# Giving out the split of a Wb tile between the two halves of a step's elementwise work

## The chip, the cores and the metric

One core of a Trainium2 chip runs the kernel. The time is device microseconds of one execution. Before the change three runs gave 1529.27, 1530.88 and 1530.9 us, with a median of 1530.88 us; less time is better. Five engines work in parallel, each through a queue of its own in program order: PE (matrix products), DVE and ACT and POOL (elementwise work), and SP, which here only issues transfers between the chip's memory and the on-chip buffers.

## The reference, cut to what matters

```python
# attention in two steps: the packed queries p attend to k and v, then q attends to the result
p_packed = sm_attn(p, k, v)
x = sm_attn(q, p_packed, p_packed)        # as 4608 tokens x 512
# first layer: d_ff = 2048
h = x @ w_in
P = a[0] + a[1] * h + a[2] * h**2 + a[3] * h**3
Q = 1.0 + abs(b[0]) * abs(h) + abs(b[1]) * h**2
x = (P / (Q + 1e-06)) @ w_out
# second layer: d_ff = 2048
h = x @ w2_in
out = (maximum(h, 0) + alpha * minimum(h, 0)) @ w2_out
```

The four weight matrices come as 64-bit floats, all else as 32-bit floats. Products are made exact enough by splitting each 32-bit operand into a rounded high part and a remainder (low part), and adding three products of parts.

## The kernel before, in words

The attention's last product is folded into the first layer's first weights: for each of the 8 batches, Wb = p_packed @ w_in, a matrix of 256 rows by 2048 columns, is made once and stored to the chip's memory (`wb_d`). The first layer then runs in 72 steps, 9 chunks of 512 tokens by 8 tiles of 256 columns: step g is chunk c = g // 8 and tile f = g % 8. A chunk takes its tokens from two batches (two "visits"), so it needs two Wb tiles in each step. Around them the loop from line 843 does, in program order:

- `emit_L1(g)` (line 591): 24 products on PE into `h`, a PSUM tile with two buffers. A buffer comes free for step g+2 when the last DVE operation of step g (L665) has read it.
- `emit_E1(g)` (line 631), the first half of the elementwise work: ACT makes `r_` = |h| (L642), `q_` (L643) and `v_` (L644) from h; POOL multiplies `q_` by `r_` (L645). For the step before, ACT copies its result into the high part of `gt` (L626) and POOL subtracts to make the low part (L627). DVE does L650 and L651 on `v_` and h.
- `emit_L2(g - 3)` (line 669): 24 products on PE of `gt` with w_out (L680), added up over a chunk in `acc`, which has one buffer.
- `emit_E2(g)` (line 653), the second half: ACT does a reciprocal square root (L657, which needs POOL's L645) and a square (L658, into h, after DVE's L651). At a chunk's end `emit_yo` copies `acc` out, one half on DVE (L614) and one on ACT (L616), and stores it on SP (L621); the next chunk's L2 waits for that. DVE ends with L663, L664, L665.
- `store_Wb()` and `next_wb(g)` (line 831).

The weights' conversion from 64 bits is hung onto these steps. A tile takes three operations on DVE (L89, L92, L95) and two on ACT (L84, L85). For w_out, steps 3 to 7 each do all three on DVE between L651 and L663, and steps 1 to 8 each split one tile (ACT L738, POOL L739) at the end of `emit_E2`. For the second layer's weights, from step 9 on, odd steps do L89 and even steps L92 and L95, at the same place; each fourth step (12, 16, 20 ...) also has four sums on POOL (L714) at its end, whose results SP stores (L719) early in the step after, ahead of a load (L707).

`next_wb(g)` holds the lines that the change touches. A Wb tile for step g+16 is asked for at the end of step g: `fetch_wb` (line 505) issues a load on SP (L511) into a staging tile `s`, one of three (tag `s2`, shared with the conversion), and the next step's `next_wb` calls `split_wb` (line 513): ACT copies the staged tile into the high part (L520), POOL subtracts for the low part (L521). 48 tiles go this way. In chunks 4 and 7 the tiles were kept from an earlier visit, and `split_wb` only issues a load of the parts on SP (L518); from step 65 on there is nothing left to split.

"Step s" below is the step whose first half is meant. The step's number isn't in the trace; `r__2042` is step 3, `r__3239` step 18.

Of the kernel before, what the change touches and what calls it, by code (L numbers as in the profile page):

```python
# [28 lines left out]
def attention_then_two_moes(ctx, tc, qT, kT, v, pT, w_in, w_out, ab, w2_in, w2_out, alpha, out):  # L29
# [69 lines left out]
    def open_pool(name, **kw):  # L99
        opened[name] = ExitStack()  # L100
        return opened[name].enter_context(tc.tile_pool(name=name, reuse_waits="tile", **kw))

    def close_pool(name):
        opened.pop(name).close()
# [87 lines left out]
    def wb_slot(n):  # L192
        return wp.tile([128, 2, 512], F32R, tag="C" if n // 8 % 2 else "B", name="wb")
# [243 lines left out]
    def store_Wb():  # L437
        while stores:
            bp, j, fc, t = stores.pop(0)
            for bi in range(2):  # L440
                nc.sync.dma_start(out=wb_d[2 * bp + bi][64 * j:64 * j + 64, 512 * fc - 512:512 * fc + 512],
                                  in_=t[64 * bi:64 * bi + 64, :])


    wb_t, whole_t, wb_q, nwb = {}, {}, [], [0]
# [46 lines left out]
    def load_a2(c):  # L492
        st = gp.tile([128, 2, CH], F32, tag="ast", name="ast", bufs=1)
        for _, b, o, n, t in chunks[c]:
            nc.sync.dma_start(out=st[:, :, o:o + n], in_=a2_d[b][:, :, t:t + n])
        a2_t[c] = st

    def split_a2(c):
        st = a2_t[c]
        t = spx.tile([128, 2, 2, CH], F32R, tag="a2t", name="a2t")  # L500
        act(t[:, 0], st, AF.Copy)
        pool.tensor_tensor(t[:, 1], st, t[:, 0], op=ALU.subtract)
        a2_t[c] = t

    def fetch_wb(n):
        v, f = divmod(n, NP)
        if v > VISITS.index(VISITS[v]):
            wb_q.append((v, f, None))
            return
        wb_q.append((v, f, s2_tile().rearrange("p (k f) -> p k f", k=2)))  # L510
        nc.sync.dma_start(out=wb_q[-1][2], in_=wb_d[VISITS[v]][:, 256 * f:256 * f + 256].rearrange("(k p) f -> p k f", p=128))  # L511

    def split_wb():
        v, f, st = wb_q.pop(0)
        whole = wb_slot(NP * v + f)
        t = whole.rearrange("p h (k f) -> p h k f", k=2)
        if st is None:
            nc.sync.dma_start(out=whole.bitcast(F32), in_=wbh_d[VISITS[v]][f])  # L518
        else:
            act(t[:, 0], st, AF.Copy)  # L520
            pool.tensor_tensor(t[:, 1], st, t[:, 0], op=ALU.subtract)  # L521
        wb_t[v, f] = t[:, 0], t[:, 1]
        whole_t[v, f] = whole

    def keep_wb(v, f):
        nc.sync.dma_start(out=wbh_d[VISITS[v]][f], in_=whole_t[v, f].bitcast(F32))
# [64 lines left out]
    def emit_L1(g):  # L591
        c, f = divmod(g, NP)
        h = psh.tile([128, 2, CH], F32, tag="h", name="h")
        for ft in range(2):
            for v, _, o, m, _ in chunks[c]:
                w = wb_t[v, f]
                n = 0
                for x, y in PASSES:
                    for k in range(2):
                        mm(h[:, ft, o:o + m], w[x][:, k, 128 * ft:128 * ft + 128], a2_t[c][:, y, k, o:o + m],  # L600
                           start=n == 0, stop=n == 5)
                        n += 1
        hps[g] = h
# [20 lines left out]
    def emit_hi(g):  # L624
        t = gt[g] = spa.tile([128, 2, 2, CH], F32R, tag="gt", name="gt", bufs=3)
        act(t[:, 0], vs[g], AF.Copy)  # L626
        pool.tensor_tensor(t[:, 1], vs.pop(g), t[:, 0], op=ALU.subtract)  # L627
# [3 lines left out]
    def emit_E1(s):  # L631


        late_step(s, "start")
        w2_step(s, "start")
        if s < NG:
            h = hps.pop(s)
            r_ = spa.tile([128, 2, CH], F32, tag="r_", name="r_", bufs=1)
            q_ = spa.tile([128, 2, CH], F32, tag="q_", name="q_", bufs=2)
            v_ = vs[s] = spa.tile([128, 2, CH], F32, tag="v_", name="v_", bufs=2)  # L640
            now[s] = h, r_, q_, v_
            act(r_, h, AF.Abs)  # L642
            act(q_, r_, AF.Identity, scale=b1, bias=b0)  # L643
            act(v_, h, AF.Identity, scale=a3, bias=a2c)  # L644
            pool.tensor_tensor(q_, q_, r_, op=ALU.mult)  # L645
        if 1 <= s <= NG:
            emit_hi(s - 1)
        late_step(s, "middle")
        if s < NG:
            dve.tensor_tensor(v_, v_, h, op=ALU.mult)  # L650
            dve.scalar_tensor_tensor(v_, in0=v_, scalar=a1c, in1=h, op0=ALU.add, op1=ALU.mult)  # L651
# [74 lines left out]
    def late_step(s, part):  # L726

        if part == "start" and s == 0:
            late_conv(1)
        elif part == "middle" and s == 0:  # L730
            w2_abs(2 - LATE)
        elif part == "dve" and (s == 0 or 3 <= s < LATE):
            late_conv(s or 2)
        elif part == "end" and 0 < s <= LATE:
            i = s - 1
            w = w2_st.pop(i - LATE).bitcast(F32)[:, 0:512]
            t = w_out_t[EARLY + i] = wo_slot(EARLY + i)
            act(t[:, 0, :], w, AF.Copy)  # L738
            pool.tensor_tensor(t[:, 1, :], w, t[:, 0, :], op=ALU.subtract)  # L739
            if s + 2 < LATE:  # L740
                w2_load(s + 2 - LATE)
            if 2 <= s < LATE - 1:
                w2_abs(s + 1 - LATE)

    def w2_step(s, part):


        n, half = divmod(s - 9, 2)
        if part == "start" and not half:
            if n % 2 == 0 and 2 <= n <= 2 * NF:  # L750
                w2_store(n - 1)
            if n >= -1:
                w2_load(n + 1)
        elif part == "dve":
            if 0 <= n < 2 * NF:
                (w2_bits if half else w2_range)(n)
        elif part == "end" and half:
            if n >= -1:
                w2_abs(n + 1)
            if n % 2 and 0 <= n < 2 * NF:  # L760
                w2_sums(n)
# [39 lines left out]
    def load_y(s):  # L801

        t0, m = SUPER[s]
        yq[s] = spy.tile([128, 2, 4, CH], F32, tag="yq", name="yq")
        for th in range(2):
            c, o = divmod(t0 + th * m, CH)
            nc.sync.dma_start(out=yq[s][:, th, :, 0:m], in_=y_d[c][:, :, o:o + m])
# [22 lines left out]

    def next_wb(g):

        while wb_q:
            split_wb()
        if g + 2 * NP < len(VISITS) * NP:
            fetch_wb(g + 2 * NP)
        c, f = divmod(g, NP)
        for i in range(3) if g == 0 else (g + 2,) if g + 2 < NP else ():
            keep_wb(0, i)
        if c == 2:  # L840
            keep_wb(3, f)

    for g in range(NG + LAG):
        if g == NG:
            close_pool("spx")
            spy = open_pool("spy", bufs=1, side="right")
            load_y(0)
        if g < NG:
            c, f = divmod(g, NP)
            if f == 1 and c + 1 < NCH:  # L850
                load_a2(c + 1)
            emit_L1(g)
            for _ in range(FILL[g] if g < len(FILL) else 0):
                emit_Wb(nwb[0])
                nwb[0] += 1
        if g == LAG - 1:
            close_pool("psw2")
            close_pool("psw")
            psa = open_pool("psa", bufs=1, space=PSUM, side="right")
        emit_E1(g)  # L860
        if g >= LAG:
            emit_L2(g - LAG)
        emit_E2(g)
        store_Wb()
        if g < NG:
            next_wb(g)
            if f == 3 and c + 1 < NCH:
                split_a2(c + 1)
        d = g - NG
        if d == -1:  # L870
            pool.tensor_scalar(nalpha, alpha_sb, -1.0, None, op0=ALU.mult)
            for n, st in enumerate((gp.tile([128, 2, CH], F32, tag="ast", name="wst", bufs=1),
                                    spa.tile([128, 2, CH], F32, tag="q_", name="wst", bufs=2))):
                for x in range(2):
                    w_load(2 * n + x, st[:, x])
        elif d >= 0:
            if d == 0:
                for n, tag in ((2, "v_"), (3, "q_")):
                    st = spa.tile([128, 2, CH], F32, tag=tag, name="wst", bufs=2)
                    for x in range(2):  # L880
                        w_load(2 * n + x, st[:, x])
            for u in range(4 * d, min(4 * d + 4, SOON)):
                w_split(u, dve)()
            if d:
                split_y(0, d - 1, y_block(0, d - 1, 0))()
# [252 lines left out]
```

## Time and profile before

| What | us |
|---|---|
| median of three runs | 1530.88 |
| lowest and highest run | 1529.27, 1530.9 |
| the profiled execution, by its own time | 1529.2 |
| its span, from first to last instruction | 1527.4 |
| PE busy | 1460.6 (96% of the span) |
| DVE busy | 1297.4 (85%) |
| ACT busy | 1030.2 (67%) |
| POOL busy | 570.4 (37%) |

The mean granted clock of PE is 0.99. All durations below are from the one profiled execution. The first layer's first product starts at 177.49 us of the span and the last step's at 803.19 us; before it lie the attention and Wb, behind it the second layer.

A row of the timeline gives the start and the duration in us, engine, line, operation and tiles, and in brackets the idle time of the engine before it with what ended it. "L" and a number is a line of the kernel.

### The profile page before, as it was taken

The numbers are of one execution on the slowest core, as the hardware profiler recorded it, in microseconds if no ns is written. First come the engines' busy times: TensorE is split into PE (matmuls) and PEld (weight loads), VectorE is DVE, ScalarE is ACT, GpSimd is POOL, SyncE is SP. The second block draws the span as 40 slices with busy tenths as digits, with TensorE's granted clock in tenths as the row PEclk, the third lists the DMA queues.
The fourth block names the chain that finished last, engine by engine and source line by source line (L and its number), as shares of the span: only waits on it lengthen the run. The fifth ranks groups of instructions, "written<-read, shape, count | busy, mean of one in ns | idle before, by whom it ended". The sixth has DMA issues, their size and how long they took to land.

```text
span 1527.4 us, 20922 instructions
## 1 busy us (share of the span) xinstructions
PE 1460.6 (96%) x7712; PEld 1204.5 (79%) x7712; DVE 1297.4 (85%) x1412; ACT 1030.2 (67%) x1194; POOL 570.4 (37%) x354
## 2 busy tenths in 40 slices
PE   4798878999999999999999999999999999999998
PEld 2444477888888888888888877888888888888898
DVE  5988789898889999899999799859966996599586
ACT  4456588988988888888886586447434743474363
POOL 3132288788787778877664610000000000000000
PEclk9899989999999999999999999999999999999999
DMA  9999944236433632424435977997567656765694
GB/s 353 342 315 295 318 154 130 67 110 200 156 111 97 211 107 84 125 97 145 145 97 194 329 241 252 376 379 273 202 209 281 194 201 213 249 193 200 218 407 169
DMA packets 151109, 322.25 MB, mean 211 GB/s; under 512 B 14816, under 2 KB 79328, under 8 KB 149984
## 3 DMA queue, kind: packets, MB, share of 16 engines
q1 hardware_dynamic: 147552, 308.34, 59.1%
q0 software_dynamic: 2304, 8.39, 1.4%
q10 hardware_dynamic: 1152, 4.19, 0.8%
q8 instruction: 61, 1.00, 0.3%
q14 instruction: 40, 0.33, 0.1%
HBM read 230.17 MB, written 90.70 MB: 210 GB/s over the span
## 4 chain that ended last, share of the span: by engine, by line
PE 55%; DVE 13%; ACT 11%; POOL 5%; issue 4%; DMA 2%; SPq 0%; POOLq 0%; ACTq 0%; DVEq 0%
PE p L1075 21%; PE p L1067 20%; PE acc L680 8%; PE h L600 5%; DVE s L92 2%; POOL s L714 1%; DVE v L910 1%; ACT h L658 1%; DVE s L89 1%; DVE s L95 1%; POOL wb L521 1%; DVE v L927 1%; ACT wb L520 1%; DVE h L664 1%; PE pw L421 1%
## 5 line engine op out<-in xcount | busy, mean ns | idle before, releaser
L680 PE MATMUL acc<-gt,wo 128*128 128x512 f32 x1728 | 406.4, 391 | 6.7 <-ACT yo L616 6.7
L680 PEld LDWEIGHTS acc<-gt,wo 128*128 128x128 f32 x1728 | 320.2, 188 | 72.4 <-ACT yo L616 8.0
L1067 PE MATMUL p<-ysp,ws 128*128 128x512 f32 (+1 forms) x1680 | 346.9, 368 | 3.0 <-ACT vsp L995 2.4
L1075 PE MATMUL p<-vsp,ws 128*128 128x512 f32 (+1 forms) x1680 | 346.5, 368 | 0.2 <-DVE vsp L996 0.2
L1067 PEld LDWEIGHTS p<-ysp,ws 128*128 128x128 f32 x1680 | 292.5, 189 | 56.8 <-ACT vsp L995 3.4
L1075 PEld LDWEIGHTS p<-vsp,ws 128*128 128x128 f32 x1680 | 292.3, 189 | 53.7 <-DVE vsp L996 1.4
L600 PEld LDWEIGHTS h<-a2t,wb 128*128 128x128 f32 x1728 | 230.6, 193 | 27.5 <-issue 16.9
L600 PE MATMUL h<-a2t,wb 128*128 128x192 f32 (+2 forms) x1728 | 236.9, 294 | 14.9 <-DVE v__1857 L665 4.7
L995 ACT ACTIVATE vsp<-v 128x1024 fp32r<-128x1024 f32 (+1 forms) x140 | 135.7, 971 | 147.7 <-PE p L1075 98.3
L996 DVE TENSOR_TENSOR vsp<-v,vsp 128x1024 fp32r<-128x1024 f32 (+1 forms) x140 | 156.1, 1115 | 32.3 <-ACT vsp L995 31.8
L910 DVE TENSOR_TENSOR v<-v,p 128x1024 f32<-128x1024 f32 (+1 forms) x100 | 110.9, 1110 | 40.6 <-PE p L1067 40.4
L927 DVE SCALAR_TENSOR_TENSOR v<-r,nalpha,v 128x512 f32<-128x512 f32 (+1 forms) x160 | 112.4, 744 | 29.7 <-ACT v L922 29.7
L921 ACT ACTIVATE r<-v 128x1024 f32<-128x1024 f32 (+1 forms) x60 | 58.3, 972 | 76.1 <-DVE v L910 75.8
L910 DVE TENSOR_TENSOR v<-v 128x1024 f32<-128x1024 f32 (+1 forms) x80 | 88.7, 1113 | 0.0
L521 POOL TENSOR_TENSOR wb<-s,wb 128x512 fp32r<-128x512 f32 x48 | 64.2, 1339 | 31.9 <-ACT wb L520 31.7
L89 DVE TENSOR_SCALAR s<-s 128x512 f32<-128x512 f32 x48 | 61.8, 1288 | 1.1 <-ACT s L84 1.1
L922 ACT ACTIVATE v<-v 128x1024 f32<-128x1024 f32 (+1 forms) x60 | 58.6, 976 | 1.9
L421 PE MATMUL pw<-w_in,pph 128*128 128x512 f32 x96 | 51.0, 642 | 8.1 <-ACT wbs L433 7.4
L92 DVE SCALAR_TENSOR_TENSOR s<-s,s 128x512 int32<-128x512 int32 x40 | 56.7, 1418 | 0.4
L935 ACT ACTIVATE v<-p 128x1024 f32<-128x1024 f32 (+1 forms) x20 | 18.8, 942 | 53.3 <-PE p L1067 53.3
L910 DVE TENSOR_TENSOR c<-c,p 128x1024 f32<-128x1024 f32 (+1 forms) x25 | 27.4, 1112 | 29.9 <-PE p L1075 29.6
L369 POOL TENSOR_TENSOR trn<-trn,mx 128x576 f32<-128x576 f32 x16 | 19.5, 1217 | 73.2 <-DVE mx L368 67.7
(1026 smaller groups left out, 2236.6 us busy)
## 6 DMA issues: line engine op xcount, KB each, us to landing
ws<-wh_d SPq DMA_DIRECT2D x224, 512.0 KB, 5.6
wh_d<-ws SPq DMA_DIRECT2D x56, 512.0 KB, 4.9
wq_d<-s SPq DMA_DIRECT2D x32, 512.0 KB, 3.7
wst<-wq_d SPq DMA_DIRECT2D x56, 256.0 KB, 3.9
wb_d<-wbs SPq DMA_DIRECT2D x48, 256.0 KB, 5.2
s<-in_w_out SPq DMA_DIRECT2D x24, 512.0 KB, 4.3
s<-wb_d SPq DMA_DIRECT2D x48, 256.0 KB, 4.0
kt<-in_kT SPq DMA_DIRECT2D x16, 576.0 KB, 6.4
```

What stands on the lines that cost most here:

```text
L89: dve.tensor_scalar(w, w, 0.0, HIGH_R, op0=ALU.max, op1=ALU.min)
L92: dve.scalar_tensor_tensor(wi, in0=wi, scalar=3, in1=low, op0=ALU.logical_shift_left, op1=ALU.bitwise_or)
L421: mm(pw, pph[bp][:, j].rearrange("p a b -> p (a b)"), w_in_t[j, fc], start=True, stop=True)
L521: pool.tensor_tensor(t[:, 1], st, t[:, 0], op=ALU.subtract)
L600: mm(h[:, ft, o:o + m], w[x][:, k, 128 * ft:128 * ft + 128], a2_t[c][:, y, k, o:o + m], start=n == 0, stop=n == 5)
L680: mm(acc[d // 2][:, d % 2, :], w[:, x, 128 * d:128 * d + 128], t[:, y, ft, :], start=f == 0 and (x, y, ft) == (0, 0, 0), stop=f == NP - 1 ...
L910: dve.tensor_tensor(o, a, b, op=op)
L927: dve.scalar_tensor_tensor(v_[:, g], in0=r[:, g], scalar=nalpha[:, f:f + 1], in1=v_[:, g], op0=ALU.mult, op1=ALU.add)
L995: act(t[:, 0, :, 0:m], src, AF.Copy)
L996: return lambda: dve.tensor_tensor(t[:, 1, :, 0:m], src, t[:, 0, :, 0:m], op=ALU.subtract)
L1067: mm(ps[:, g, 0:m], w[:, g, x, 128 * k:128 * k + 128], ysp[s, i](z, k), start=not onto and q == 0, stop=q == 5, skip_group_check=again)
L1075: mm(ps[:, d, 0:m], w[:, g, x, 128 * d:128 * d + 128], t[:, z, g, 0:m], start=not onto and n == 0 and g == 0 and q == 0, stop=n == 3 and g ...
```

## The change

`split_wb` is no longer called at the head of `next_wb`, at a step's end, but behind `emit_E1` of the same step, ahead of `emit_L2` and `emit_E2`. The fetch of the next tile stays where it was.

```diff
     def next_wb(g):
 
-        while wb_q:
-            split_wb()
         if g + 2 * NP < len(VISITS) * NP:
             fetch_wb(g + 2 * NP)
         c, f = divmod(g, NP)
@@ -858,6 +856,8 @@
             close_pool("psw")
             psa = open_pool("psa", bufs=1, space=PSUM, side="right")
         emit_E1(g)
+        while wb_q:
+            split_wb()
         if g >= LAG:
             emit_L2(g - LAG)
         emit_E2(g)
```

## Rows read from the trace of the kernel before

**Rows 1.** The page, busy tenths of PE in 40 slices of the span.
```profile
PE   4798878999999999999999999999999999999998
```
**Rows 2.** Waits of PE, 176 to 850 us: total, times, longest.
```profile
PE acc L680 <- ACT yo L616: 6.7, 6, 1.3
...
PE h L600 <- DVE v__2858 L665: 0.5, 1, 0.5
```
**Rows 3.** Chain of work that ended last, 200 to 272 us: start, duration, what.
```profile
204.17 4.83 DMA s<-wb_d
...
209.62 1.02 ACT r__2042 L642
...
263.92 3.10 PE h L600 x24
```
**Rows 4.** Timeline of SP's queue ahead of that fetch: the stores of Wb.
```profile
201.06 3.06 SPq L441 DMA_DIRECT2D wb_d<-wbs  x4
```
**Rows 5.** Timeline of ACT, step 2 and the start of step 3.
```profile
202.95 1.05 ACT L626 ACTIVATE gt<-v__1926 128x1024 fp32r<-128x1024 f32 x1
204.49 1.15 ACT L657 ACTIVATE r__1986<-q__1987,qc 128x1024 f32<-128x1024 f32 x1 [0.50 <-POOL q__1987 L645]
...
207.75 0.68 ACT L85 ACTIVATE s<-s 128x512 int32<-128x512 uint8 x1
209.09 0.63 ACT L520 ACTIVATE wb<-s 128x512 fp32r<-128x512 f32 x1 [0.65 <-DMA s<-wb_d]
```
**Rows 6.** Timeline of DVE, the conversion in step 7.
```profile
256.26 1.50 DVE L89 TENSOR_SCALAR s<-s 128x512 f32<-128x512 f32 x1
257.80 0.69 DVE L92 SCALAR_TENSOR_TENSOR s<-s,s 128x512 int32<-128x512 int32 x1
258.52 1.66 DVE L95 SCALAR_TENSOR_TENSOR s<-s,s 128x512 int32<-128x512 int32 x1
```
**Rows 7.** Timeline of POOL beside Rows 6.
```profile
255.07 2.41 POOL L627 TENSOR_TENSOR gt<-v__2298,gt 128x1024 fp32r<-128x1024 f32 x1 [0.59 <-ACT gt L626]
258.10 1.53 POOL L739 TENSOR_TENSOR wo<-s,wo 128x512 fp32r<-128x512 f32 x1 [0.62 <-ACT wo L738]
```
**Rows 8.** Line 95, from 215 to 262 us and from 270 to 830 us: duration min/median/max in ns.
```profile
L95 DVE SCALAR_TENSOR_TENSOR s<-s,s x5: 1664/1672/1683, 217.9 to 258.5; 128x512 int32<-128x512 int32 x5
L95 DVE SCALAR_TENSOR_TENSOR s<-s,s x32: 691/692/695, 284.8 to 818.3; 128x512 int32<-128x512 int32 x32
```
**Rows 9.** Timeline of DVE, L92 of step 16 and L89 of step 17.
```profile
335.44 1.86 DVE L92 SCALAR_TENSOR_TENSOR s<-s,s 128x512 int32<-128x512 int32 x1
...
344.09 0.90 DVE L89 TENSOR_SCALAR s<-s 128x512 f32<-128x512 f32 x1
```
**Rows 10.** Timeline of POOL beside Rows 9.
```profile
334.35 2.40 POOL L627 TENSOR_TENSOR gt<-v__3008,gt 128x1024 fp32r<-128x1024 f32 x1
338.11 0.75 POOL L714 TENSOR_TENSOR s<-s 128x256 f32<-128x256 f32 x1 [1.36 <-DVE s L95]
...
341.04 1.30 POOL L521 TENSOR_TENSOR wb<-s,wb 128x512 fp32r<-128x512 f32 x1
...
344.65 2.60 POOL L627 TENSOR_TENSOR gt<-v__3080,gt 128x1024 fp32r<-128x1024 f32 x1
```
**Rows 11.** Timeline of ACT, the square roots of steps 17 and 18, the copy of `acc`.
```profile
344.74 1.15 ACT L657 ACTIVATE r__3166<-q__3167,qc 128x1024 f32<-128x1024 f32 x1 [2.02 <-POOL q__3167 L645]
...
352.22 1.15 ACT L657 ACTIVATE r__3239<-q__3240,qc 128x1024 f32<-128x1024 f32 x1 [0.46 <-POOL q__3240 L645]
...
354.42 1.01 ACT L616 ACTIVATE yo<-acc 128x1024 f32<-128x1024 f32 x1
```
**Rows 12.** Timeline of PE, the next chunk's first L2.
```profile
355.48 5.74 PE L680 MATMUL acc<-gt,wo 128*128 128x512 f32 x24 [0.91 <-ACT yo L616]
```
**Rows 13.** Timeline of SP's queue: the fetch for step 18's split.
```profile
347.31 1.38 SPq L511 DMA_DIRECT2D s<-wb_d  x1
```
**Rows 14.** Line 511 from 347.3 to 348.6 us: how long that fetch took to land.
```profile
DMA to landing us min/median/max: 5.2/5.2/5.2
```

## The prediction

> **What bounds the kernel now.** I read the busy slices first, then PE's waits, the chain that ended last, and the queues around single steps. From the eighth slice on PE is nearly always busy [rows 1]: the first layer's steady part and the second layer run at PE's pace, and only PE's idle time can be won there. That time is small: PE waits six times at a chunk's border for ACT's copy of `acc`, 6.7 us in all, and a few tenths at a time for a free `h` [rows 2]. (A border that waits is 1.2 to 1.6 us longer than its neighbours, start of L1 to start of L1.) The chunk's first steps are different. From 204 to 264 us the chain runs through a fetched Wb tile, ACT's step 3, and then DVE without a break until PE's L1 at 263.92 [rows 3]. There steps 3 to 7 convert w_out, DVE has some 10 us of work in a step, more than PE, and PE waits for DVE. So what delays that chain delays everything behind it.
>
> **The change, part by part.** Nothing is added or removed: 48 copies on ACT (L520), 48 subtractions on POOL (L521) and 16 reloads on SP (L518) move forward by half a step. ACT now does the copy behind L626 and ahead of L657, POOL the subtraction behind L627 and ahead of everything of the step's end. A copy takes 0.52 us of ACT's time; where ACT waits for POOL's product, that wait hides it, and the step's end is 0.5 us shorter. The reloads are moved ahead of the `acc` stores on SP, into tiles whose readers are done; I cost them at nothing, and if that cover went they would hold SP for 0.4 us each. The staging tile comes free earlier too; nobody waits for that, as SP's other waits come first.
>
> *The new wait, step 2.* A copy at a step's end had a whole step for its fetch to land; in the middle it has half. In step 2 the fetch was issued at 204.17, behind four stores of Wb, and took 4.83 us [rows 3, 4]. At the old place ACT waited 0.65 us for it [rows 5]. At the new one ACT is there at 204.0, when L626 ends (202.95 plus 1.05), and waits until 209.1. Queued behind it on ACT are L657, L658, a w_out copy, L84 and L85: from 204.49 to about 208.3 (0.57 us after L85's start) they took 3.8 us [rows 5], which lay ahead of the wait and now lie behind it. Step 3's |h| thus starts at 213.4 in place of 209.62, and it is on the chain [rows 3]. The issue doesn't come sooner: it stands behind stores that the change leaves alone. Cost: **3.8 us**.
>
> *DVE and POOL, steps 3 to 7.* L89 starts at 256.26 while POOL's L627 is running, takes 1.50 us and ends 0.3 us after L627 does. L92 then takes 0.69, L95 1.66, as POOL's L739, which was waiting (1.53 us for what else takes 1.30), got in between L92 and L95 [rows 6, 7]. So these DVE operations and POOL's subtractions shut each other out. All five steps show it: L95 takes 1.66 to 1.68 us there, and 0.69 in all 32 later ones, where POOL had nothing queued [rows 8]. Who wins when both are queued is also shown: at the end of a POOL operation DVE's waiting one goes first (L89 at 344.09 ended in 0.90 us although L627 was queued, and L627 took 2.60 in place of 2.40 [rows 9, 10]); between two DVE operations POOL's waiting one goes first [rows 6, 7]. In the new order L521 is queued right behind L627, its copy long done: it will go in between L89 and L92, and L739 between L92 and L95 as before. L89 to L95 then costs another 1.66 less 0.69, about 1.0 us, with a little from the later square 1.07. Steps 3, 5, 6 and 7 pay it; in step 4 a chunk's `a2t` split already made L89 wait (2.46 us), and that room swallows it. Cost: 4 x 1.07 = **4.3 us**. It could be 0 (POOL loses the race) or 5 x 1.3 = 6.5 (each L521 at full length); I take the value that the five L95 show. The L1 of step 9, at 263.92, then starts 8.1 us late, and PE-bound work follows it: nothing gives that back.
>
> The Trainium skill, SBUF — State Buffer, calls the port pair that DVE and GpSimd (POOL) share an exclusive lock, held for a whole instruction, while the loser fully blocks. By that rule each L521 would cost its full 1.30 us and this term would be 5.2 in place of 4.3 us; the 0.97 us of L95 speaks for the smaller value.
>
> *The steady steps.* In every fourth step POOL's sums wait 1.36 us for L95, and L521 (1.30 us) and the next step's product stood behind them [rows 10]; ACT's L657 then waits 2.02 us [rows 11]. That gap looks made for L521. But by the same race it goes between L92 and L95, L95 ends 1.0 us later, the sums too, and the product comes only 1.3 - 1.0 = 0.3 us earlier. Three borders (steps 34, 50, 58) gain 0.3 us each. Step 42 had no wait and has none; step 10 hangs on DVE's step 9 and loses 0.1.
>
> At two borders the fetch comes too late. The one for step 18 is issued at 347.31, behind the stores of the sums and a load, and took 5.2 us: landed at 352.5 [rows 13, 14]. Sums 1.0 later make that 353.5; the copy ends at 354.0, L657 starts there, not at 352.22, and the copy of `acc` at 356.2, not at 354.42 [rows 11]. PE, which already waited 0.91 [rows 12], waits 1.8 more. Step 26 repeats the pattern (issued 415.63, landed 422.0, L657 at 422.61) and gives 1.0. The borders together: 1.8 + 1.0 + 0.1 - 0.9 = **2.0 us**.
>
> Last, all even steps with a split end 1.0 us later on DVE. PE's L1 two steps on needs that `h`. In most steps it has 0.6 to 1.6 us to spare, but in the second sums step of a chunk (12, 20, 28, 44, 52) only 0.1 to 0.4, or none: PE already waits there in places [rows 2]. Each loses some 0.8 us and gets about 0.4 back, since small waits behind it vanish; step 12, which is also behind a late fetch, loses 0.9 net. 4 x 0.35 + 0.9 = **2.3 us**, with bounds of 0 and 5.
>
> Sum: 3.8 + 4.3 + 2.0 + 2.3 = 12.4 us. Against the profiled execution's own 1529.2 us (a span of 1527.4 and 1.8 around it) that is 1541.6; the median of the runs lies 1.7 us above that execution, so the forecast is **1543 us**.
>
> **Rivals.** (a) *The subtraction fills POOL's gap.* If DVE keeps L92 and L95 together, L521 runs while POOL would idle, and the product behind the sums is 1.3 us earlier. Borders 34, 50 and 58 then lose their waits (1.1 + 1.6 + 1.6 us), the small waits for `h` give some 1.5, steps 18 and 26 cost 0.9 and 0; against 3.8 us at step 2 the net is about -1 us: 1530, not slower. It decides at the end of L627 in an even step, by whether L95 stays at 0.69 us. For it speaks that POOL idles there; against it the five L95 of 1.66. (b) *Only the wait of step 2 bites.* POOL finds room in steps 3 to 7 and gain and loss cancel later: 1530.9 + 3.8 = 1535, slower by 0.25%. (c) *(a), and step 2 costs nothing*, since the fetch lands early or DVE had room in step 3: 1530.9 - 5 = 1526. Against it: the chain goes through that very fetch [rows 3].
>
> **How the numbers follow.** The forecast has 0.67 (from 1537 to 1549 by its bounds), (b) 0.13, (a) 0.13, (c) 0.05, and 0.02 is left. A measurement of this kernel can tell about 0.2%, 3 us, from no change. Faster takes (c) and some of (a): 0.08; the same, most of (a) and a part of (b): 0.15; slower the rest: 0.77. A range from 1530 to 1549 leaves out (c), half of (a) and some 0.05 above.
>
> **What would show it.** Right: in the trace after, ACT's L520 of step 2 waits some 5 us, and L657 of that step starts near 209.6; L95 takes about 1.7 us in even steps, and L92 in steps 3 to 7 too; L1 of step 9 starts near 272; the square root of step 18 waits for a transfer. Wrong: L95 still at 0.69 us in even steps (then (a)), or L1 of step 9 near 264 (then the early terms fall). A sum that is wrong in size would most likely be so in the two last terms, which were carried from row to row over several steps.

## The result and the profile after

The changed kernel takes 1539.17 us (median of 6 runs, 1538.14 to 1541.95); the kernel before, measured again beside it, 1530.89 us (6 runs). The medians are 8.3 us apart. The ratio on record is 1.0064, with a 95% interval of 1.0054 to 1.0074, which makes it 9.8 us: slower, clear of the noise. The forecast was 1543, with 1530 to 1549 as its range. The profiled execution after took 1541.95 us, the longest of the six and 12.75 more than the one before. Of that, 0.65 us lay ahead of the first layer, and 2.15 us arose in step 0, where L95 (at 186.12 us) ran into POOL's L645 and took 2.73 us, which no other trace of this study shows. So stretches are compared from the end of step 1's L665 on.

| What | before | after |
|---|---|---|
| end of step 1's L665 to L1 of step 9, us | 61.51 | 69.01 |
| L1 of step 9 to L1 of step 71, us | 539.26 | 541.85 |
| L1 of step 71 to the end, us | 724.21 | 724.05 |
| DVE busy, us | 1297.4 | 1328.5 |
| PE busy, us | 1460.6 | 1461.5 |

Three quarters of the loss lie in steps 2 to 8, and nothing of it in the second layer. The new wait stands where it was looked for. ACT's queue in step 2 (start, duration, operation, and in brackets the idle time before it):

```profile
205.55 1.04 ACT L626 ACTIVATE gt<-v__1926 128x1024 fp32r<-128x1024 f32 x1
211.86 0.63 ACT L520 ACTIVATE wb<-s 128x512 fp32r<-128x512 f32 x1 [5.27 <-DMA s<-wb_d]
212.39 1.14 ACT L657 ACTIVATE r__1986<-q__1987,qc 128x1024 f32<-128x1024 f32 x1
...
215.61 0.67 ACT L85 ACTIVATE s<-s 128x512 int32<-128x512 uint8 x1
216.17 1.01 ACT L642 ACTIVATE r__2042<-h 128x1024 f32<-128x1024 f32 x1
```

and SP's queue ahead of it, the fetch behind the stores as before:

```profile
203.87 3.00 SPq L441 DMA_DIRECT2D wb_d<-wbs  x4
206.92 1.18 SPq L511 DMA_DIRECT2D s<-wb_d  x1
```

Before, ACT waited 0.65 us for this fetch, with all of step 2's own work on ACT already done [rows 5]. Now it waits 5.27 us, and that work, 3.8 us from L657 to the |h| of step 3, comes after the wait. The time for a fetch to land is what it was (206.92 to 211.77, 4.85 us).

DVE and POOL in step 7, the rows that answer to [rows 6, 7]:

```profile
265.60 1.49 DVE L89 TENSOR_SCALAR s<-s 128x512 f32<-128x512 f32 x1
267.12 1.66 DVE L92 SCALAR_TENSOR_TENSOR s<-s,s 128x512 int32<-128x512 int32 x1
268.82 1.67 DVE L95 SCALAR_TENSOR_TENSOR s<-s,s 128x512 int32<-128x512 int32 x1
```
```profile
264.41 2.40 POOL L627 TENSOR_TENSOR gt<-v__2298,gt 128x1024 fp32r<-128x1024 f32 x1 [1.94 <-ACT gt L626]
266.76 1.48 POOL L521 TENSOR_TENSOR wb<-s,wb 128x512 fp32r<-128x512 f32 x1
268.20 1.75 POOL L739 TENSOR_TENSOR wo<-s,wo 128x512 fp32r<-128x512 f32 x1
```

L521 got in between L89 and L92 and made L92 1.66 us long, where it took 0.69. Line 92 before, from 215 to 262 us, and after, from 222 to 272 us (min/median/max in ns):

```profile
L92 DVE SCALAR_TENSOR_TENSOR s<-s,s x5: 692/694/703, 217.2 to 257.8; 128x512 int32<-128x512 int32 x5
...
L92 DVE SCALAR_TENSOR_TENSOR s<-s,s x5: 1664/1668/1672, 223.7 to 267.1; 128x512 int32<-128x512 int32 x5
```

Line 95 after, from 222 to 272 us and from 290 to 845 us, beside [rows 8]:

```profile
L95 DVE SCALAR_TENSOR_TENSOR s<-s,s x5: 1665/1669/1671, 225.4 to 268.8; 128x512 int32<-128x512 int32 x5
L95 DVE SCALAR_TENSOR_TENSOR s<-s,s x32: 691/1664/1678, 294.7 to 831.2; 128x512 int32<-128x512 int32 x32
```

In the steady steps the median L95 went from 0.692 to 1.664 us: all 20 in steps that have a subtraction are long, the others are as before. What the change gave there can be seen beside [rows 10] and [rows 11]: POOL's sums in step 16 and the product of step 17, then ACT in steps 17 and 18, then PE at that border.

```profile
348.22 1.76 POOL L521 TENSOR_TENSOR wb<-s,wb 128x512 fp32r<-128x512 f32 x1
350.62 0.74 POOL L714 TENSOR_TENSOR s<-s 128x256 f32<-128x256 f32 x1 [0.63 <-DVE s L95]
...
353.53 2.42 POOL L645 TENSOR_TENSOR q__3167<-q__3167,r__3166 128x1024 f32<-128x1024 f32 x1
```
```profile
355.98 1.15 ACT L657 ACTIVATE r__3166<-q__3167,qc 128x1024 f32<-128x1024 f32 x1 [0.24 <-POOL q__3167 L645]
...
364.23 0.63 ACT L520 ACTIVATE wb<-s 128x512 fp32r<-128x512 f32 x1 [0.94 <-DMA s<-wb_d]
364.76 1.14 ACT L657 ACTIVATE r__3239<-q__3240,qc 128x1024 f32<-128x1024 f32 x1
...
366.90 1.01 ACT L616 ACTIVATE yo<-acc 128x1024 f32<-128x1024 f32 x1
```
```profile
367.96 5.73 PE L680 MATMUL acc<-gt,wo 128*128 128x512 f32 x24 [1.50 <-ACT yo L616]
```

The sums start 0.6 us later against PE's L1 of step 16, as they wait for the longer L95, yet POOL's product (L645) and ACT's L657 come 0.65 us earlier, as no L521 stands ahead of them. ACT's wait behind the sums fell from 2.02 to 0.24 us, but one step later ACT waits 0.94 us for the fetch, and PE's wait at the border went up, from 0.91 to 1.50 us [rows 12]. Over all borders PE's wait for the copy of `acc` fell a little, while waits for `h` came up. PE's waits, 176 to 865 us (total, times, longest), beside [rows 2]; the three for `h` are those of steps 3, 7 and 12, which before were 1.0, 1.3 and 0.2 us:

```profile
PE acc L680 <- ACT yo L616: 5.6, 6, 1.5
PE h L600 <- DVE v__2044 L665: 3.5, 1, 3.5
...
PE h L600 <- DVE v__2380 L665: 2.3, 1, 2.3
...
PE h L600 <- DVE v__2774 L665: 1.7, 1, 1.7
```

### The profile page after: what moved, and what is told of

It reads as the page before. It is cut to its first block, busy times and chain, and to the rows that moved or that the text cites. A ratio compares the mean times of both kernels' runs of the same rounds, so it can differ in the third digit from the quotient of the medians.

```text
span 1540.1 us, 20925 instructions
## 1 busy us (share of the span) xinstructions
PE 1461.5 (95%) x7712; PEld 1206.0 (78%) x7712; DVE 1328.5 (86%) x1412; ACT 1030.1 (67%) x1194; POOL 580.8 (38%) x354
## 4 chain that ended last, share of the span: by engine, by line
PE 54%; DVE 21%; issue 6%; ACT 4%; DMA 2%; SPq 0%; POOL 0%; ACTq 0%; DVEq 0%
PE p L1075 20%; PE p L1067 20%; PE acc L680 8%; PE h L600 5%; DVE h L664 3%; DVE s L92 2%; DVE s L95 2%; DVE s L89 2%; DMA s<-wb_d 1%; DVE v L910 1%; DVE v L927 1%; DVE ws L793 1%; DVE vsp L996 1%; DMA wst<-wq_d 0%; DMA wq_d<-s 0%
## 5 line engine op out<-in xcount | busy, mean ns | idle before, releaser
L600 PE MATMUL h<-a2t,wb 128*128 128x192 f32 (+2 forms) x1728 | 237.7, 295 | 26.9 <-DVE v__1857 L665 6.8
L600 PEld LDWEIGHTS h<-a2t,wb 128*128 128x128 f32 x1728 | 231.2, 194 | 40.1 <-issue 30.0
L521 POOL TENSOR_TENSOR wb<-s,wb 128x512 fp32r<-128x512 f32 x48 | 75.9, 1581 | 3.4 <-ACT wb L520 3.2
L89 DVE TENSOR_SCALAR s<-s 128x512 f32<-128x512 f32 x48 | 72.0, 1499 | 0.9 <-ACT s L84 0.7
L92 DVE SCALAR_TENSOR_TENSOR s<-s,s 128x512 int32<-128x512 int32 x40 | 59.8, 1495 | 0.4
L95 DVE SCALAR_TENSOR_TENSOR s<-s,s 128x512 int32<-128x512 int32 x40 | 54.1, 1354 | 1.4
```

Source lines behind the costliest of these rows:

```text
L89: dve.tensor_scalar(w, w, 0.0, HIGH_R, op0=ALU.max, op1=ALU.min)
L92: dve.scalar_tensor_tensor(wi, in0=wi, scalar=3, in1=low, op0=ALU.logical_shift_left, op1=ALU.bitwise_or)
L95: dve.scalar_tensor_tensor(o, in0=high, scalar=-(1 << 31), in1=wi, op0=ALU.bitwise_and, op1=ALU.bitwise_or)
```

## The experiments

Two causes were on record for steps 2 to 8: the wait for the fetch in step 2, and the race between L521 and the conversion on DVE. Theory: both cost, and their costs add up. Rival 1: the wait makes the whole loss. Rival 2: the race does. Each kernel is compared with the kernel before on the same chip. "First" is the stretch from the end of step 1's L665 to the L1 of step 9, "second" that from there to the L1 of step 71.

| Kernel | ratio to before (95%) | first, us | second, us |
|---|---|---|---|
| before | 1 | 61.51 | 539.26 |
| changed | 1.0064 (1.0054 to 1.0074) | 69.01 | 541.85 |
| e1, copy moved alone | 1.0035 (1.0023 to 1.0048) | 65.45 | 540.17 |
| e2, subtraction moved alone, 3 staging tiles | 1.0144 (1.0130 to 1.0159) | 65.69 | 556.39 |
| e5, the same with 4 staging tiles | 1.0020 (1.0011 to 1.0030) | 65.20 | 539.03 |
| e3, changed but for step 2 | 1.0025 (1.0014 to 1.0036) | 65.01 | 539.75 |
| e6, copy alone, but for step 2 | 1.0005 (0.9995 to 1.0015) | 61.56 | 540.69 |
| e7, changed, fetch ahead of stores | 1.0035 (1.0022 to 1.0048) | 65.74 | 541.11 |
| e4, changed from step 9 on | 1.0012 (1.0003 to 1.0022) | 61.29 | 541.94 |
| e9, e4 without the border steps | 1.0009 (1.0000 to 1.0018) | 61.70 | 540.16 |
| e8, subtraction put off after sums | 0.9930 (0.9914 to 0.9945) | 61.01 | 529.37 |

The stretches come from one profile of each kernel. How far they can be trusted shows where programs agree: e4, e8 and e9 have the program of before up to step 9, and their first stretches are 61.01 to 61.70 us; e3, e4 and e7 have the changed program from step 9 on, and with the changed kernel their second stretches are 539.75 to 541.94 us. So the first is good to some 0.5 us, the second to some 2 us.

In the kernels with a function `sub_wb` (e1, e2, e5, e6, e8) lines behind it are 7 or a few more higher: L527 is the copy L520, L649 the |h| L642, L607 is L600; the subtraction L521 is L518 there.

**e1: ACT's copy alone.** The copy is given out in the middle, the subtraction at the end.

```diff
             act(t[:, 0], st, AF.Copy)
-            pool.tensor_tensor(t[:, 1], st, t[:, 0], op=ALU.subtract)
+            wb_low.append((t, st))
...
     def next_wb(g):
+        sub_wb()          # pool.tensor_tensor(t[:, 1], st, t[:, 0], op=ALU.subtract)
```

> Only ACT's copy (L520) and the reloads move to the middle of the step; POOL's subtraction stays at the step's end, as before. This keeps the wait of step 2 and takes away the race for the port. Theory (wait of step 2 plus race): L520 of step 2 waits some 5 us, L95 takes 0.69 us in even steps from step 9 on, the L1 of step 9 starts about 4 us later than in the kernel before; in all 3 to 6 us slower than before (ratio 1.002 to 1.004). Rival 1, the wait of step 2 alone makes the whole loss: 8 us slower (1.005). Rival 2, the race alone makes it: no slower than before (1.000).

Measured: 1.0035, and the first stretch 3.9 us longer. ACT in step 2, then the L1 of step 9:

```profile
207.35 0.63 ACT L527 ACTIVATE wb<-s 128x512 fp32r<-128x512 f32 x1 [4.28 <-DMA s<-wb_d]
...
211.66 1.00 ACT L649 ACTIVATE r__2042<-h 128x1024 f32<-128x1024 f32 x1
```
```profile
266.32 3.09 PE L607 MATMUL h<-a2t,wb 128*128 128x256 f32 x24 [1.04 <-DVE v__2380 L672]
```

The wait alone costs 3.9 us, as reckoned (3.8), and it isn't the whole: rival 1 falls, and so does rival 2, which wanted nothing here. One sign was missed. Line 92 from 215 to 272 us, and line 95 from 272 to 830 us:

```profile
L92 DVE SCALAR_TENSOR_TENSOR s<-s,s x5: 692/694/695, 219.2 to 260.2; 128x512 int32<-128x512 int32 x5
```
```profile
L95 DVE SCALAR_TENSOR_TENSOR s<-s,s x32: 691/693/1687, 286.8 to 821.6; 128x512 int32<-128x512 int32 x32
```

L92 is at 0.69 us in the early steps, as it should be. But L95 isn't at 0.69 in all even steps from 9 on: in the ten without sums (10, 14, 18 and so on to 54) it takes 1.64 to 1.69 us, in e6 too. There the copy is done so early that the subtraction, though still given out at the step's end, gets in between L92 and L95 (in step 14 right behind the subtraction for `gt`, L634). So e1 and e6 are free of the new race in the first stretch alone; their second stretches, 0.9 and 1.4 us longer than before, hold a part of it and the late fetches.

**e2 and e5: POOL's subtraction alone.** The copy stays at the end of a step; the subtraction stands behind the next step's L627. In e2 this keeps a staging tile half a step longer.

```diff
         emit_E1(g)
+        sub_wb()
```

> Only POOL's subtraction (L521) moves: ACT's copy stays at the step's end, the subtraction stands behind L627 of the next step, where the changed kernel has it. This keeps the race and takes away the wait of step 2. Theory: L520 of step 2 waits under 1 us, L95 takes 1.67 us in even steps, L92 1.67 us in the steps that convert w_out, the L1 of step 9 starts 3 to 5 us later than before, some 2 us more are lost in the steady steps; in all 4 to 7 us slower than before (1.003 to 1.0045). Rival 1, the wait alone: no slower (1.000). Rival 2, the race alone: 8 us slower (1.005).

Measured: 1.0144, far outside all three. The first stretch is as the theory has it (4.2 us longer), but the second is 17 us longer. The longest row of ACT's and POOL's waits there, 270 to 830 us:

```profile
ACT s L84 <- POOL wb L518: 31.7, 20, 1.9
```

Twenty times ACT's L84 of the conversion waited for a staging tile that the put-off subtraction still read: a wait that the experiment had made itself. With a fourth tile it is gone:

```diff
-        return gp.tile([128, 512], F32, tag="s2", name="s2", bufs=3)
+        return gp.tile([128, 512], F32, tag="s2", name="s2", bufs=4)
```

To make room, a tile that only fills space is cut from 120 to 8 columns.

> As the kernel that moved POOL's subtraction alone behind the next step's L627, but with four staging tiles in place of three (and a filler tile shrunk to make room), so that ACT's L84 no longer waits for a staging tile. In the run with three, ACT waited 35.7 us in all for it. Theory (that wait made the loss of the steady steps; the race costs 3.5 to 4.2 us up to step 9 and nearly nothing later): the L1 of step 9 stays 3.5 to 4.2 us late, the stretch from there to step 71 comes back from +17 us to within 2 us of before; in all 3 to 6 us slower than before (1.002 to 1.004). Rival, the race itself costs the steady steps 10 us and more: still 1.010 or above.

Measured: 1.0020. ACT's copy in step 2 is at 208.27 without a wait of note. Line 92 from 215 to 272 us, and line 95 from 272 to 830 us:

```profile
L92 DVE SCALAR_TENSOR_TENSOR s<-s,s x5: 1655/1672/1676, 216.3 to 259.7; 128x512 int32<-128x512 int32 x5
```
```profile
L95 DVE SCALAR_TENSOR_TENSOR s<-s,s x32: 691/1665/1679, 287.7 to 820.9; 128x512 int32<-128x512 int32 x32
```

The race is there in full, in the early steps and the steady ones. In the early steps, where DVE sets the pace, it costs 3.7 us. In the steady steps L95 is 1 us longer 20 times over, and the second stretch is no longer than before (539.03 against 539.26). That isn't because the race is free there: the table under e9 shows that a loss of 2.0 us behind the sums steps stands against 1.9 us won at the borders.

**e3, e6: step 2 left as before.** e3 is the changed kernel with `while wb_q and (g != 2)` in the middle and the rest of the queue at the old place; e6 does the same to e1, and so has neither the wait nor the new race up to step 8.

> The changed kernel, but step 2 alone gives out its split at the step's end, as before. Theory: the L1 of step 9 starts 3.8 us earlier than in the changed kernel, and the whole is 3 to 5 us faster than that (4 to 5 us slower than before, 1.003). Rival 1, the wait alone: back at the time of before (1.000). Rival 2, the race alone: as slow as the changed kernel (1.005 to 1.006).

> ACT's copy alone moves to the middle, but in step 2 it stays at the end; POOL's subtraction is at the step's end everywhere. Both costs are taken away: the wait of step 2 and the race. Theory, the two add up and there is no third: the L1 of step 9 starts as in the kernel before (within 0.7 us), the time is within 0.1% of before. Rival, moving the copy costs something of its own in steps 3 to 8: 2 us slower or more.

Measured: e3 1.0025, its first stretch 3.5 us longer, 4.0 less than in the changed kernel; e6 1.0005, its first stretch 61.56 us, as before. So the two add up: 3.9 for the wait (e1), 3.5 to 3.7 for the race (e3, e5), 7.5 for both (changed), 0.05 for neither (e6). Within the 0.5 us to which this stretch is good, there is no third cause in these steps.

**e7: the fetch ahead of the stores.** In step 1 `next_wb` goes ahead of `store_Wb`; the rest is the changed kernel.

```diff
-        store_Wb()
+        if g != 1:
+            store_Wb()
         if g < NG:
             next_wb(g)
+            if g == 1:
+                store_Wb()
```

> The changed kernel, but in step 1 the fetch is issued ahead of the four stores of Wb, not behind them. Nothing else differs. Theory, step 2 waits for the landing of that fetch and for nothing else: the fetch is issued some 3 us earlier, L520 of step 2 waits 1 to 3 us in place of 5, the L1 of step 9 starts 2 to 4 us earlier than in the changed kernel; 4 to 6 us slower than before (1.003 to 1.004). Rival, the position in step 2 costs by itself (ACT's order, POOL's order): as slow as the changed kernel (1.0055 or above).

Measured: 1.0035, the first stretch 3.3 us shorter than in the changed kernel. SP's queue, then ACT in step 2:

```profile
201.07 0.38 SPq L511 DMA_DIRECT2D s<-wb_d  x1
...
202.05 4.74 SPq L441 DMA_DIRECT2D wb_d<-wbs  x4
```
```profile
205.80 0.63 ACT L520 ACTIVATE wb<-s 128x512 fp32r<-128x512 f32 x1 [2.29 <-DMA s<-wb_d]
```

The fetch, issued 3.1 us earlier, lands 3 us earlier, and the loss shrinks by that. It is the landing for which step 2 pays, not the place of the copy.

**e4 and e9: the steady steps alone.** e4 moves the split from step 9 on; e9 leaves the steps f = 2 and f = 3 out of that too.

```diff
+        while wb_q and (g >= 9 and g % 8 not in (2, 3)):     # e9; e4: g >= 9
+            split_wb()
```

> The split moves to the middle only from step 9 on; steps 1 to 8 stand as before. What is left is the steady part: L95 at 1.67 us in even steps, late fetches at the borders of steps 18 and 26, earlier products behind the sums. Theory: 1 to 4 us slower than before (1.001 to 1.0025), the L1 of step 9 as before. If only what happens up to step 9 costs anything, it is 1.000; if POOL's gap is really filled, 3 to 6 us faster (0.997).

> As the kernel that gives out the split in the middle from step 9 on, but the two steps at each chunk's border (f = 2 and f = 3, where the acc stores hold up the fetch) give it out at the end, as before. Theory (what the steady steps lose is the wait for late fetches at the borders; the race costs nothing there): the stretch from the L1 of step 9 to that of step 71 falls from 541.9 us to 538 to 540, and the whole is 0 to 2 us faster than before (0.9985 to 1.0000). Rival, the loss comes from the race in even steps: as slow as with the border steps, 1.001 or above.

Measured: e4 1.0012, its second stretch 2.7 us longer, about as the changed kernel's. In e4 ACT waits 1.29, 1.11, 1.20, 0.85 and 0.56 us for a fetch in steps 11, 18, 19, 27 and 43. e9, without these, has 540.16 us, 1.8 less than e4, but still 0.9 more than before and outside the 538 to 540 that I gave; its ratio, 1.0009 (1.0000 to 1.0018), is outside my 0.9985 to 1.0000 too and doesn't rule out the rival's 1.001. By time e4 and e9 can't be told apart.

Nor does the difference of 1.8 us show what the fetches cost, for 1.6 of it is something else. PE in e4, the first L2 behind the border of step 18, and the granted clock from 358 to 359 us (the last number but two):

```profile
356.13 7.36 PE L680 MATMUL acc<-gt,wo 128*128 128x512 f32 x24 [1.70 <-ACT yo L616]
```
```profile
358.00:359.00 1.00, 1.00 (x4) 0.81 (x3) 0.97 (x2) 0.97 (x2) 0.00 (x0) 0.50 0.97 310
```

Behind a wait of 1.70 us the granted clock stood at 0.50 (1.2 of 2.4 GHz) for some 3.4 us, and the product took 7.36 us in place of 5.74 [rows 12]. In the changed kernel's trace it stayed at 1.00 there, behind a wait of 1.50 us.

The starts of PE's L1 tell the parts of the second stretch from each other. A border is the stretch from one L1 to the next in which PE waits for the copy of `acc` (from the L1 of steps 11, 19, 27, 35, 51 and 59). The other column adds up four steps each, from the L1 of the sums steps 12, 20, 28, 44 and 52, where PE waits for `h`. All in us against the kernel before:

| Kernel | six borders | behind five sums steps | second stretch |
|---|---|---|---|
| changed | -1.3 | +3.7 | +2.6 |
| e3 | -1.9 | +2.2 | +0.5 |
| e4 | +0.7 (+1.6 by the clock) | +1.9 | +2.7 |
| e5 (race, no late fetch) | -1.9 | +2.0 | -0.2 |
| e9 (race, no late fetch) | -2.5 | +3.4 | +0.9 |
| e8 | -6.5 | -2.8 | -9.9 |

So in the steady steps the moved subtraction both costs and gains: it lengthens the sums steps and shortens the borders. The late fetches come on top. The longer ACT waits for one in step 11, the more the four steps from 12 on lose: 1.8 us at a wait of 2.02 (changed), 1.1 at 1.29 (e4), 1.1 at 1.06 (e7), 0.6 at 0.77 (e3), against 0.7 and 0.4 without such a wait (e9, e5). With a spread of some 2 us from trace to trace, as large as the whole term, the shares can't be told more exactly.

**e8: what the gap behind the sums is worth.** Made from the kernel before: the split stays at the step's end, and only in steps with sums on POOL is the subtraction put off behind L627 of the next step.

```diff
     def next_wb(g):
         while wb_q:
             split_wb()            # act(...); wb_low.append((t, st))
+        if g < 12 or g % 4:
+            sub_wb()
...
         emit_E1(g)
+        sub_wb()
```

> Made from the kernel before, the split at the step's end: only the subtraction of a step that has sums on POOL (step 12 and every fourth after it) is put off behind L627 of the next step. The product behind the sums then no longer waits 1.3 us for L521, and no L521 stands between L92 and L95. Theory (in the steady steps it is POOL's order behind the sums that makes the borders wait): L657 behind the sums waits 0.7 us in place of 2.0, the waits of PE for the copy of acc fall from 6.7 us to under 3 us; 4 to 7 us faster than before (0.9955 to 0.9975). Rival, the borders hang on DVE or on a transfer: no faster (0.999 to 1.001).

Measured: 0.9930 (0.9914 to 0.9945), 1519.08 us: faster than both kernels, by more than expected. POOL in steps 16 and 17, ACT in 17, then PE at the border of step 18:

```profile
340.76 2.41 POOL L652 TENSOR_TENSOR q__3166<-q__3166,r__3165 128x1024 f32<-128x1024 f32 x1
343.13 2.41 POOL L634 TENSOR_TENSOR gt<-v__3080,gt 128x1024 fp32r<-128x1024 f32 x1
345.48 2.75 POOL L518 TENSOR_TENSOR wb<-s,wb 128x512 fp32r<-128x512 f32 x2
```
```profile
343.20 1.15 ACT L664 ACTIVATE r__3165<-q__3166,qc 128x1024 f32<-128x1024 f32 x1 [0.76 <-POOL q__3166 L652]
```
```profile
354.22 5.66 PE L687 MATMUL acc<-gt,wo 128*128 128x512 f32 x24
```

The sums go straight to the product that ACT waits for, the subtractions (two here, step 16's and step 17's own) run behind it, and no L521 stands between L92 and L95. PE's waits for `acc`, 176 to 850 us:

```profile
PE acc L687 <- ACT yo L623: 1.3, 1, 1.3
```

Five of the six border waits are gone, and nearly all the small waits for `h` with them: of some 12 us that PE lost before between steps 9 and 71 (by the starts of L1, against its undisturbed step), 9.9 are won.

## Why the prediction was right, and where its sum was off

- *What bounds the kernel.* Right: nothing changed behind the first layer, the loss lies where DVE sets PE's pace, and what e8 wins in the steady part, 9.9 of some 12 us, is PE's idle time.
- *The wait of step 2, 3.8 us.* Right: 3.9 us in e1, and e7 moves it with the landing of the fetch.
- *The race in steps 3 to 7, 4.3 us.* Right in kind: L521 went in between L89 and L92, DVE took L89 first, and L92 paid 0.97 us. A little too large: 3.5 us in e3, 3.7 in e5. I had added 0.1 us a step for the later square, which the traces don't show; the ends of L665 slip by 1.0 us a step in steps 5, 6 and 7. By the rule of the Trainium skill (SBUF — State Buffer, section Terms), that the shared pair is held for the full instruction and the loser fully blocks, the term would be an estimated 5.2 us. The trace agrees that DVE and POOL shut each other out, but not on the full price: in step 7 L521's row begins 0.33 us before L89's ends, and L92's ends 0.54 us after L521's, less than the 0.69 it takes alone. The rows overlap at both edges, and 0.97 of 1.30 us is left; why they overlap isn't shown.
- *The borders, 2.0 us.* This step failed, in its sign: the trace has 1.3 us won, and of the other two traces in the table with this program from step 9 on, e3 has 1.9 won and e4, without its slow clock, 0.9. Step 18 did lose to the late fetch, 0.6 us on PE, not 1.8; step 26 gained 0.5 where I had it lose 1.0, as its fetch landed 0.8 us ahead of ACT's copy. Both were carried on the assumption that the sums, and with them SP's stores and the fetch, come 1.0 us later, from the 1.0 us of L95. Since ACT was ahead in even steps, L92 could start earlier, and in step 16 the sums began 0.6 us late against PE, and the fetch landed no later at all. The other four borders gained 1.4 us where I had 0.8.
- *The even steps, 2.3 us.* Right in kind and within its bounds, but too small for this trace. The L1 of steps 14, 22, 30 and 46 waited for `h`, as forecast, and the five groups lost 3.7 us, in e3 and e4 2.2 and 1.9. In e5, with the race and no late fetch, each lost 0.4 us, near the 0.35 that I had. What I had too small is step 12 behind the late fetch: 1.8 us, not 0.9.
- *The sum.* 12.4 us forecast; 10.1 by the stretches of the trace (7.5 and 2.6), 9.8 by the ratio, 8.3 by the medians. Most of what is too much sits in the two last terms (4.3 against 2.6), as the prediction's end allowed for. That they came so near in sum is luck in part: the borders were put 3.3 us too high, the even steps 1.4 too low.
- *The rivals.* (a) falls: L95 stands at 1.66 us in even steps, and POOL's product behind the sums came, ahead of the borders, 0.4 to 0.7 us earlier, not 1.3. (b) falls: both costs are there. (c) falls with them. What (a) hoped for is real, though: e8 gets it by another order.

## What to carry to other kernels

A producer that is moved earlier in a step takes its own wait with it: look at what is queued behind the moved instruction, and at when its input lands, not only at the gap that it should fill. A gap on one engine in which it waits for another engine isn't free if work put there shuts out that very engine: here POOL's subtraction delayed the DVE operation for which POOL was waiting. To shorten a queue ahead of a critical operation, put work off behind it, as e8 does, and check that the buffer it keeps isn't the next wait, as in e2. A stretch that is as long as before can hold a cost and a gain that cancel, as in e5: compare it step by step, and look at the granted clock before a slow step is put down to a wait, as in e4.

## What the runs showed of the hardware that wasn't expected

Who gets through when DVE and POOL shut each other out is orderly enough to be read ahead: at the end of a POOL operation the waiting DVE operation goes first, between two DVE operations the waiting POOL operation does. That was read from a few rows before, and it held throughout: in the changed kernel all of the five L92 and five L95 of steps 3 to 7 took 1.66 to 1.67 us, and all 20 L95 in later steps with a subtraction 1.64 to 1.68. Not expected was that the subtraction falls into the same place without being moved, once its input is ready early (the ten L95 in e1 and in e6). Chance remains where neither waits: in step 0 of the profiled execution after, L95 came at 186.12 us, 0.55 us behind L645, and took 2.73 us; in the one before it came 0.17 us ahead of L645 and took 0.69.

In some of the traces PE's granted clock fell for a few microseconds in the middle of steady work; in e4 and e7 a step took 1.5 to 1.6 us longer by that. Behind the wait of 1.70 us in e4 it was at 0.50 from 357 to 359 us, and in e7, behind a wait of 2.31 us at the L1 of step 9, it was at 0.50 from 270 to 272 us and that L1 took 4.60 us in place of 3.09. What brings the fall about isn't shown: behind the wait of 2.29 us at the same L1 of the changed kernel the product took 3.08 us.
